# Four edits around one PE-bound mLSTM kernel: quadrants for scaled q, plain transposes for x, a later place for w_out's combinations, one pass on GpSimd

## The chip, the cores and the metric

The kernel runs on 1 core of one Trainium2 chip. The metric is the device time of one execution in microseconds (us), shorter is better; where several runs are at hand, their median. The core has TensorE (PE in the profile, with its weight loads as PEld), VectorE (DVE), ScalarE (ACT), GpSimd (POOL) and SyncE (SP), which issues most DMA transfers. Each engine takes its instructions strictly in its own order, and engines wait for one another through semaphores.

## The reference

Two blocks follow each other. The first is an mLSTM cell with 4 batches, 8 heads, 768 tokens and a head dimension of 40; the second is a feed-forward layer with a leaky ReLU, from 320 to 2048 to 320, on all 3072 tokens.

```python
for t in range(S):
    m_new = max(f[t] + m, i[t]); f_stab = exp(f[t] + m - m_new); i_stab = exp(i[t] - m_new); m = m_new
    C = f_stab * C + i_stab * outer(v[t], k[t])
    n = f_stab * n + i_stab * k[t]
    y[t] = sigmoid(o_gate[t]) * (C @ q[t]) / max(abs(n @ q[t]), 1.0)
x = y.transpose(0, 2, 1, 3).reshape(3072, 320)
h = x @ w_in
out = maximum(0.01 * h, h) @ w_out
```

`w_in` and `w_out` arrive as 64-bit floats. The kernel computes in 32-bit floats, so it narrows the weights itself.

## The kernel before

**Chunks, steps, groups.** The tokens are cut into 6 chunks of 128 (`c`), and a *step* `s = 4 * c + b` is one chunk of one batch. The cell of chunk `c` and the feed-forward layer of chunk `c - 1` (a *group* `g = c - 1` of 4 x 128 = 512 tokens) run side by side. In the cell, q times k gives scores, the scores are weighted with exponentials of the gates, and both the weighted scores and the scaled q (q times the gate's decay) are multiplied into a tile that holds v and the running state.

**Order.** Except for SP, whose transfers have an order chain of their own, the order on every engine is the order of the Python calls. `first_chunk` (L1125) writes out chunk 0: steps 0 and 1, then steps 2 and 3, each with `gate` (L690), `u_x` (L778) and `prepare_step` (L176, GpSimd memsets). The loop at L1244 then walks, per chunk, over the units `ffs[i]` of the feed-forward layer; between them it places the cell's units at fixed places (`place` for chunk 1, `pairs` for the later chunks). Generators are advanced a few instructions at a time: `now` (the narrowing of the weights), `sums` (sums of w_in), `mixes` (combinations of w_out), `lazy` (exponentials), `fine` (transposes of q and k).

**Chunk 1** (steps 4 to 7). For each step `u_split` (L571) turns k and q by matmuls with the identity into the tile `tk`; `u_parts` (L645) first calls `split_qs` (L562), which turns the scaled q (the tile `y`) into `tq`, copied by ScalarE into the tile `qn`; then come the scores `sd` (L662, L667), which VectorE multiplies with the weights into the other half of `qn` (L672) and adds to the state (L643). `u_plain` (L701) multiplies `qn` by v and state into `hN` (L710), takes the denominators, and makes `x` on VectorE (L721) and GpSimd (L726). `ahead(s + 1)` then puts `prep_qs` (L523), `state_next` (L639), `prep_vu` (L514) of the next step and `prep_mask` (L486) of the one after it on GpSimd. When all four steps are done, four `u_x` turn `x` into `xT`, 64 features by tokens in 5 slots of 128 rows: four transposes into the tile `xt`, two matmuls with a 64-column output into `xe`, and three copies.

**fp32 on PE.** In the traces an fp32 matmul shows as two PE instructions, a transpose as one: the 16 matmuls of `split_qs` are 32 in each step, the four transposes of `u_x` are 4 and its two matmuls 4. `split_qs` uses two quadrants of the array in turn (rows 0-63 to columns 64-103, rows 64-127 to columns 0-39); `u_split` uses all four.

**Weights.** `narrow_weights(n)` (L264) makes 32-bit floats of w_in (n = 0 to 3) and w_out (n = 4 to 11, 640 numbers in each of 128 rows) in six passes: two on ScalarE (L272, L273), four on VectorE (bounds L274, shift L277, sign L280, add L281). Those of n = 2 to 11 are drawn in chunk 1 through `now`. Group 0 uses w_in and w_out plainly (L804, L826). The later groups use a scheme with 7 block products instead of 8: `fast_firsts` (L961, matmuls at L977) and `fast_units` (L850, matmuls at L861). It needs sums of w_in (`sums_of_weights`, L932), of x (`sums_of_x`, L951) and of w_out: `mixed_weights` (L220) makes `t3` (L224), the right half of w_out's low rows in place (L225), `t2` (L226) and `t4` (L227).

**PSUM.** Two pools of 4 banks each: `mm` for the feed-forward layer, `c` for the cell.

Of the kernel before, what the change touches and what calls it, by code (L numbers as in the profile page):

```python
# [19 lines left out]
def kernel(  # L20
# [28 lines left out]
    P = 128  # L49
# [6 lines left out]
    D1 = D + 1  # L56
    QW = 32
    DB = D // 2
    V1 = DB + 1
    TB = P // QW  # L60
    SL = P // 2
# [202 lines left out]
    def narrow_weights(n):  # L264

        if not wide:
            return
        raw, dst = raws.pop(n)
        words = raw.bitcast(U32).rearrange("p (c two) -> p c two", two=2)
        lo, hi = words[:, :, 0], words[:, :, 1]  # L270
        d = dst.bitcast(U32)
        yield nc.scalar.activation(dst, hi.bitcast(F32), AF.Abs)  # L272
        yield nc.scalar.activation(lo, lo, AF.Copy, scale=2.0**-29)  # L273
        yield nc.vector.tensor_scalar(  # L274
            dst, dst, scalar1=2.0**-15, scalar2=122879.9921875, op0=ALU.max, op1=ALU.min,
        )
        yield nc.vector.tensor_scalar(  # L277
            d, d, scalar1=0x07FFFFFF, scalar2=3, op0=ALU.bitwise_and, op1=ALU.logical_shift_left,
        )
        yield nc.vector.scalar_tensor_tensor(d, in0=hi, scalar=0xC0000000, in1=d, op0=ALU.bitwise_and, op1=ALU.bitwise_or)  # L280
        yield nc.vector.tensor_tensor(d, d, lo, op=ALU.add)  # L281
# [8 lines left out]
    def gates(c):  # L290


        m0 = m0s.get(c)
        n = P if c == 0 else BH
        fc, il = (f0[:], i0[:]) if c == 0 else (fi[c][:, 0, :], fi[c][:, 1, :])
        F = wk.tile([n, P], F32, name="F", bufs=1)
        nc.vector.tensor_tensor_scan(F[:], fc, zeros[:n].to_broadcast([n, P]), 0.0, op0=ALU.add, op1=ALU.add)
        if c > 0:
            il_t = wk.tile([BH, P], F32, name="il", bufs=1)
            nc.vector.tensor_scalar(il_t[:], il, scalar1=m0[:], scalar2=None, op0=ALU.subtract)  # L300
            il = il_t[:]
        m = wk.tile([n, P], F32, name="m", bufs=1)
        nc.vector.tensor_tensor_scan(m[:], fc, il, -1e30 if c == 0 else 0.0, op0=ALU.add, op1=ALU.max)
        a = early[:, 2, :] if c == 0 else wk.tile([n, P], F32, name="a", bufs=1)
        nc.vector.tensor_tensor(a[:], F[:], m[:], op=ALU.subtract)
        bu = wk.tile([n, 3, P], F32, name="bu", bufs=1)
        nc.vector.tensor_tensor(bu[:, 0, :], il, F[:], op=ALU.subtract)
        if c + 1 < NB:
            m1 = wk.tile([BH, 1], F32, name="m0")
            if c == 0:  # L310
                nc.vector.tensor_copy(m1[:], m[:BH, P - 1 :])
            else:
                nc.vector.tensor_tensor(m1[:], m0[:], m[:, P - 1 :], op=ALU.add)
            m0s[c + 1] = m1
        if c > 0:
            na = wk.tile([BH, 1], F32, name="na")
            nc.vector.tensor_tensor(na[:], m[:, SL - 1 : SL], F[:, SL - 1 : SL], op=ALU.subtract)
        bus[c] = bu, a, (na if c > 0 else None)
# [243 lines left out]
    def split_qs(s):  # L562

        tq = [psc.tile([P, H, SL], F32, name=f"tq{u}", tag="c") for u in range(2)]
        for h in range(H):
            for u, toks, rows in subs(s):
                nc.tensor.matmul(tq[u][rows, h, :], lhsT=st[s]["qs"][toks, h], rhs=ident[toks, toks], start=True, stop=True)  # L567
        for u, toks, rows in subs(s):
            nc.scalar.copy(mixed(s)[rows, u], tq[u][rows])

    def u_split(s):  # L571

# [117 lines left out]
    def gate(s):  # L690

        d = st[s]
        d["x"] = wk.tile([P, Dm], F32, name="x")
        x3 = d["x"][:].rearrange("p (h d) -> p h d", d=D)
        nc.vector.scalar_tensor_tensor(
            x3, in0=d["o"].rearrange("p (h d) -> p h d", d=D), scalar=1.0, in1=d["pa"][:, :, :D],
            op0=ALU.add, op1=ALU.mult,
        )
        nc.vector.tensor_tensor(x3, x3, d["den"][:].unsqueeze(2).to_broadcast([P, H, D]), op=ALU.mult)

    def u_plain(s):  # L701

        c, b = divmod(s, B)
        d = st[s]
        prep_o(s)
        hN = psc.tile([P, H, 2, V1], F32, name="hN", tag="c")
        m = mixed(s)
        for h in range(H):
            for u in range(2):
                nc.tensor.matmul(  # L710
                    hN[ts(u, SL), h].rearrange("p k d -> p (k d)"), lhsT=m[:, u, h, :], rhs=S_v[s % NL][:, u, h, :, :V1],
                    start=True, stop=True,
                )
        state_next(s, 1)
        den = wk.tile([P, H], F32, name="den")
        denominators(den[:], hN[:, :, 0, DB])
        if b < 2:
            d["x"] = wk.tile([P, Dm], F32, name="x")[:]
        else:
            d["x"] = wk.tile([P, H, D1], F32, name="hn")[:].rearrange("p h d -> p (h d)")[:, :Dm]  # L720
        nc.vector.scalar_tensor_tensor(  # L721
            d["x"].rearrange("p (n d) -> p n d", d=DB), in0=natural(s, 2).rearrange("p h (k d) -> p (h k) d", d=DB), scalar=1.0,
            in1=hN[:].rearrange("p h k d -> p (h k) d")[:, :, :DB], op0=ALU.add, op1=ALU.mult,
        )
        x3 = d["x"].rearrange("p (h d) -> p h d", d=D)
        nc.gpsimd.tensor_tensor(x3, x3, den[:].unsqueeze(2).to_broadcast([P, H, D]), op=ALU.mult)  # L726
        state_add(s, 1)

    def u_mix(s):
# [48 lines left out]
    def u_x(s, last=None):  # L778

        c, b = divmod(s, B)  # L780
        d = st[s]
        if b == 0:
            st["xT", c] = wk.tile([P, KC, GT], F32, name="xT", bufs=1)
        xT = st["xT", c]
        xt = psc.tile([P, KC - 1, P], F32, name="xt", tag="c")
        xe = psc.tile([P, P], F32, name="xe", tag="c")
        x, tok = d["x"], ts(b, P)
        for n, at in enumerate((0, P, DP, DP + P)):
            nc.tensor.transpose(xt[:, n, :], x[:, at : at + P], ident[:])  # L789
        for r, at in enumerate((KF * P, 0)):  # L790
            nc.tensor.matmul(xe[ts(r, DP), :], lhsT=x[:, at : at + DP], rhs=ident[:], start=True, stop=True)
        nc.scalar.copy(xT[:, :2, tok], xt[:, :2, :])  # L792
        nc.scalar.copy(xT[:, 2, tok], xe[:])
        (last or nc.scalar.copy)(xT[:, 3:, tok], xt[:, 2:, :])
        if c > 0:
            del st[s]

# [418 lines left out]
    with tc.manual_schedule(engines={E.PE, E.DVE, E.Activation, E.Pool}):  # L1216
# [20 lines left out]
        late = {}  # L1237
        masks = {0: (2, 3), 14: (4, 5)}
        pairs = (1, 1, 3, 3, 13, 13, 17, 17, 17)
        sums = sums_of_weights()  # L1240
        N1 = 14
        now = (None for n in range(2, QN + NF // 2) for _ in narrow_weights(n))
        chores, slow = [], []
        for c in range(1, NB + 1):  # L1244
# [6 lines left out]
            for i in range(n_ff):  # L1251
# [20 lines left out]
                        del fine[min(fine)]  # L1272
                if c == 1 and i >= 24:
                    run(sums, 3)
                if c == 1 and i == n_ff - 2:
                    mixes = mixed_weights()
                if c == 1 and i >= n_ff - 2 or c == 2 and 11 <= i < N1 - 1:
                    next(mixes)
                if i == n_ff - 1 and c < NB:
                    sums_of_x(c)  # L1280
# [74 lines left out]
```

## Time and profile before

| | us |
|---|---|
| median of 3 runs | 490.45 (490.13 to 492.2) |
| profiled execution | 489.68 |
| its span (first to last instruction) | 487.9 |
| PE busy | 476.3 (98% of the span) |
| DVE busy | 334.8 (69%) |
| ACT busy | 202.8 (42%) |
| POOL busy | 176.3 (36%) |

| group of instructions | count | mean ns of one |
|---|---|---|
| L567 PE `tq` (scaled q, 64x40) | 128 | 218 |
| L569 ACT copy `tq` to `qn`, 40x512 | 8 | 579 |
| L789 PE `xt` from `x` | 24 | 377 |
| L791 PE `xe` from `x` | 24 | 399 |
| L274 DVE bounds of w_out, 128x640 | 8 | 679 |
| L224 to L227 DVE combinations of w_out, 128x1280 | 1 each | 1494, 1897, 1485, 2460 |

The matmuls of PE overlap one another, so the time that a stage of PE takes is read from the chain or the timeline (from the start of its first instruction to the start of the next stage), not from the mean of one. The profiled execution is 1.78 us longer than its span, and 0.77 us below the median of the runs. A clock of 1.00 in the profile is the full TensorE clock; the mean granted over the whole execution was 0.983.

### The profile page before, as it was taken

Reading aid. Unit: us, or ns where it says so; the run is one execution under the profiler, and the core shown is the slowest. Engines: PE = TensorE matmul, PEld = TensorE weight load, DVE = VectorE, ACT = ScalarE, POOL = GpSimd, SP = SyncE. Lnnn points to the kernel's source line nnn. Section 1 sums busy time; section 2 is a strip of 40 time slices with the busy share of each in tenths; the row PEclk is TensorE's granted clock in tenths of the full one; section 3 lists DMA queues with packets and bytes.
Section 4 is the critical chain, followed back from the end, with each engine's and each line's share of the span. In section 5 each row is a group of like instructions: output and inputs, shape, how many; then the busy total and the mean of one; then the engine's idle time right before and its main releaser. Section 6 shows DMA issues by size and latency. Waiting matters only on the chain.

```text
span 487.9 us, 14080 instructions
## 1 busy us (share of the span) xinstructions
PE 476.3 (98%) x5685; PEld 428.5 (88%) x5685; DVE 334.8 (69%) x557; ACT 202.8 (42%) x488; POOL 176.3 (36%) x233
## 2 busy tenths in 40 slices
PE   8798999999999999999999999999999999999997
PEld 6676998777678899989899988899989899988997
DVE  3756567699999798888687878688647677104631
ACT  3662498864335631256420345520346411153210
POOL 4311305552376222785113784113773003700020
PEclk9887899999999999999999999999999999999999
DMA  9999686878651584675763775764865212100001
GB/s 122 172 200 210 121 223 179 207 138 173 145 142 28 126 170 83 148 167 122 173 137 88 172 150 123 181 124 90 174 146 126 60 48 68 68 1 1 1 0 55
DMA packets 165040, 59.31 MB, mean 122 GB/s; under 512 B 128560, under 2 KB 155760, under 8 KB 164976
## 3 DMA queue, kind: packets, MB, share of 16 engines
q1 hardware_dynamic: 124944, 51.23, 47.3%
q10 hardware_dynamic: 40032, 7.18, 9.0%
q8 instruction: 45, 0.74, 0.6%
q14 instruction: 19, 0.16, 0.1%
HBM read 51.68 MB, written 6.70 MB: 120 GB/s over the span
## 4 chain that ended last, share of the span: by engine, by line
PE 90%; DMA 4%; SPq 4%; DVE 1%; issue 1%; ACTq 0%; ACT 0%
PE ph L977 32%; PE po L861 32%; PE po L826 7%; PE ph L804 7%; SPq L91 4%; PE pT L740 3%; PE sd L662 3%; DMA acts<-in_moe_w_in_dram 2%; DMA raw<-in_moe_w_in_dram 1%; PE sd L667 1%; PE hN L710 1%; PE tk L581 1%; PE tq L567 1%; PE xt L789 1%; DMA f<-in_f_gate_dram 0%
## 5 line engine op out<-in xcount | busy, mean ns | idle before, releaser
L861 PE MATMUL po<-w_out,acts 128*128 128x160 f32 x640 | 89.1, 300 | 0.0
L861 PEld LDWEIGHTS po<-w_out,acts 128*128 128x128 f32 x640 | 87.3, 190 | 0.6 <-ACT acts L1002 0.3
L977 PE MATMUL ph<-xT,w_in 64*128 64x256 f32 x720 | 82.7, 378 | 0.0
L977 PEld LDWEIGHTS ph<-xT,w_in 64*128 64x128 f32 x720 | 69.3, 187 | 8.8 <-issue 1.1
L1006 DVE TENSOR_TENSOR acts<-acts,ph 128x512 f32<-128x512 f32 x60 | 38.4, 683 | 43.4 <-PE ph L977 43.4
L861 PE MATMUL po<-raw,acts 128*128 128x160 f32 x480 | 66.4, 300 | 0.0
L861 PEld LDWEIGHTS po<-raw,acts 128*128 128x128 f32 x480 | 65.4, 190 | 0.3
L1010 ACT COPY acts<-ph 128x512 f32<-128x512 f32 x60 | 32.1, 586 | 49.1 <-PE ph L977 49.1
L639 POOL TENSOR_TENSOR S<-S,f 40x336 f32<-40x336 f32 x36 | 29.5, 819 | 61.2 <-PE pT L740 26.2
L1002 ACT ACTIVATE acts<-acts 128x1024 f32<-128x1024 f32 x30 | 31.7, 1056 | 44.1 <-DVE acts L1006 33.7
L486 POOL TENSOR_TENSOR w<-w,i 128x512 f32<-128x512 f32 x20 | 26.7, 1340 | 59.5 <-DMA w<-a_dr 41.3
L494 ACT ACTIVATE w<-w,gT 128x64 f32<-128x64 f32 x160 | 41.7, 339 | 10.5 <-DMA w<-a_dr 5.7
L804 PE MATMUL ph<-xT,w_in 64*128 64x256 f32 x320 | 38.5, 395 | 0.7 <-DVE w_in L281 0.7
L672 DVE TENSOR_TENSOR qn<-w,sd 64x512 f32<-64x512 f32 x40 | 27.3, 683 | 15.6 <-ACT acts L1010 4.5
L826 PE MATMUL po<-w_out,acts 128*128 128x320 f32 x128 | 37.1, 441 | 0.0
L977 PE MATMUL ph<-acts,w 64*128 64x256 f32 x320 | 36.6, 381 | 0.0
L804 PEld LDWEIGHTS ph<-xT,w_in 64*128 64x128 f32 x320 | 32.5, 196 | 4.4 <-PE dC L619 0.8
L754 POOL TENSOR_TENSOR xb<-xb,den 128x320 f32<-128x320 f32 x16 | 11.6, 727 | 61.1 <-DVE xb L751 61.1
L977 PEld LDWEIGHTS ph<-acts,w 64*128 64x128 f32 x320 | 30.4, 187 | 3.7
L826 PEld LDWEIGHTS po<-w_out,acts 128*128 128x128 f32 x128 | 23.5, 190 | 9.8 <-issue 1.0
L959 POOL TENSOR_TENSOR acts<-xT 64x256 f32<-64x256 f32 (+1 forms) x30 | 25.5, 862 | 13.0 <-ACT xT L792 9.9
L894 POOL TENSOR_TENSOR y<-y,raw 128x160 f32<-128x160 f32 x10 | 9.4, 944 | 55.8 <-DVE acts L896 45.3
(173 smaller groups left out, 780.0 us busy)
## 6 DMA issues: line engine op xcount, KB each, us to landing
rb<-in_k_dram SPq DMA_DIRECT2D x64, 80.0 KB
rb<-in_q_dram SPq DMA_DIRECT2D x64, 80.0 KB
rb<-in_o_gate_dram SPq DMA_DIRECT2D x64, 80.0 KB
ea<-a_dr SPq DMA_DIRECT2D x32, 128.0 KB
raw<-in_moe_w_out_dram SPq DMA_DIRECT2D x6, 640.0 KB
w<-a_dr ACTq DMA_DIRECT2D x24, 128.0 KB
xT<-x_dr SPq DMA_DIRECT2D x32, 96.0 KB
x_dr<-x SPq DMA_DIRECT2D x64, 40.0 KB
```

Of the source, the lines that this page charges most:

```text
L486: nc.gpsimd.tensor_tensor(w, w, cm2.unsqueeze(1).to_broadcast([P, H, SL]), op=ALU.add)
L494: yield nc.scalar.activation(w[:, h, :], w[:, h, :], AF.Exp, bias=gT[c][:, 0, bh : bh + 1], scale=1.0)
L639: nc.gpsimd.tensor_tensor(new, old, g, op=ALU.mult)
L672: nc.vector.tensor_tensor(mixed(s)[toks, u], w[toks], bank[1 - u][toks], op=ALU.mult)
L804: nc.tensor.matmul(ph[r][:, cols], lhsT=w_row(r, slot, j), rhs=xT[DP * r : DP * (r + 1), slot, cols], start=(slot == 0), stop=(slot == KC ...
L826: nc.tensor.matmul(po[n][:], lhsT=acts[:, f, ts(n, P)], rhs=w_out[:, f, :], start=(f == 0), stop=(f == NF - 1),)
L861: nc.tensor.matmul(bank[:], lhsT=left[:, f, :], rhs=right[:, f, :], start=f == 0, stop=f == KH - 1)
L959: nc.gpsimd.tensor_tensor(to, left, right, op=ALU.subtract)
L977: nc.tensor.matmul(bank[r][:, e, :], lhsT=left(r)[rows, e], rhs=right(r)[rows], start=first and e == 0 and m == 0, stop=e == 1 and m == le ...
L1002: nc.scalar.activation(to, z, AF.Prelu, alpha=0.01)
L1006: nc.vector.tensor_tensor(to[:, 2 * r : 2 * r + 2], to[:, 2 * r : 2 * r + 2], bank[r], op=ALU.add)
L1010: nc.scalar.copy(to[:, 2 * r : 2 * r + 2], bank[r])
```

## The change

1. **`split_qs`:** heads 0 to 3 go to the two quadrants as before, heads 4 to 7 to the other two; the heads are taken in the order 0, 4, 1, 5, 2, 6, 3, 7. ScalarE makes four copies of 40x256 instead of two of 40x512.
2. **`u_x`:** `x` becomes 64 columns wider, and GpSimd copies the first 64 columns behind the last (in `gate` and in `u_plain`). Then slot 2 of `xT` is a plain transpose like the others: five transposes, the first two into one bank (`xt`, now called `low`), three into another (`xe`, now `high`), and two copies, of 128x256 and 128x384.
3. **`narrow_weights`:** for w_out (n = 4 to 11) the pass of the bounds is issued on GpSimd; for w_in it stays on VectorE.
4. **`mixed_weights`:** the first two combinations move from the last two units of group 0 to units 3 and 4 of group 1; the other two stay at units 11 and 12 of group 1.
5. **`gates`:** one subtraction works in place; the tile `il` falls away.

```diff
-        yield nc.vector.tensor_scalar(
+        yield (nc.gpsimd if n >= QN else nc.vector).tensor_scalar(
             dst, dst, scalar1=2.0**-15, scalar2=122879.9921875, op0=ALU.max, op1=ALU.min,
         )
...
-            il_t = wk.tile([BH, P], F32, name="il", bufs=1)
-            nc.vector.tensor_scalar(il_t[:], il, scalar1=m0[:], scalar2=None, op0=ALU.subtract)
-            il = il_t[:]
+            nc.vector.tensor_scalar(il, il, scalar1=m0[:], scalar2=None, op0=ALU.subtract)
...
-        for h in range(H):
+        for h in (0, 4, 1, 5, 2, 6, 3, 7):
             for u, toks, rows in subs(s):
-                nc.tensor.matmul(tq[u][rows, h, :], lhsT=st[s]["qs"][toks, h], rhs=ident[toks, toks], start=True, stop=True)
+                to = rows if h < 4 else slice(SL * u, SL * u + D)
+                nc.tensor.matmul(tq[u][to, h, :], lhsT=st[s]["qs"][toks, h], rhs=ident[toks, toks], start=True, stop=True)
         for u, toks, rows in subs(s):
-            nc.scalar.copy(mixed(s)[rows, u], tq[u][rows])
+            for hs, to in ((slice(0, 4), rows), (slice(4, H), slice(SL * u, SL * u + D))):
+                nc.scalar.copy(mixed(s)[rows, u, hs], tq[u][to, hs])
...
         nc.vector.tensor_tensor(x3, x3, d["den"][:].unsqueeze(2).to_broadcast([P, H, D]), op=ALU.mult)
+        nc.gpsimd.tensor_copy(x[:, Dm:], x[:, :DP])
...
         nc.gpsimd.tensor_tensor(x3, x3, den[:].unsqueeze(2).to_broadcast([P, H, D]), op=ALU.mult)
+        nc.gpsimd.tensor_copy(x[:, Dm:], x[:, :DP])
...
-        xt = psc.tile([P, KC - 1, P], F32, name="xt", tag="c")
-        xe = psc.tile([P, P], F32, name="xe", tag="c")
-        x, tok = d["x"], ts(b, P)
-        for n, at in enumerate((0, P, DP, DP + P)):
-            nc.tensor.transpose(xt[:, n, :], x[:, at : at + P], ident[:])
-        for r, at in enumerate((KF * P, 0)):
-            nc.tensor.matmul(xe[ts(r, DP), :], lhsT=x[:, at : at + DP], rhs=ident[:], start=True, stop=True)
-        nc.scalar.copy(xT[:, :2, tok], xt[:, :2, :])
-        nc.scalar.copy(xT[:, 2, tok], xe[:])
-        (last or nc.scalar.copy)(xT[:, 3:, tok], xt[:, 2:, :])
+        x, xT, tok = st[s]["x"], st["xT", c], ts(b, P)
+        low = psc.tile([P, 2, P], F32, name="xt", tag="c")
+        high = psc.tile([P, KC - 2, P], F32, name="xe", tag="c")
+        for t, n, at in ((low, 0, 0), (low, 1, P), (high, 1, DP), (high, 2, DP + P), (high, 0, 2 * P)):
+            nc.tensor.transpose(t[:, n, :], x[:, at : at + P], ident[:])
+        nc.scalar.copy(xT[:, :2, tok], low[:])
+        (last or nc.scalar.copy)(xT[:, 2:, tok], high[:])
...
-        sums = sums_of_weights()
+        sums, mixes = sums_of_weights(), mixed_weights()
...
-                if c == 1 and i == n_ff - 2:
-                    mixes = mixed_weights()
-                if c == 1 and i >= n_ff - 2 or c == 2 and 11 <= i < N1 - 1:
+                if c == 2 and i in (3, 4, 11, 12):
                     next(mixes)
```

## The prediction

> **What bounds the kernel now.** I read the page's first part, then PE's waits, then the chain of waits in order of time, then the timelines of POOL and DVE at step 5, where the change adds a wait.
>
> ```profile
> PE 476.3 (98%) x5685; PEld 428.5 (88%) x5685; DVE 334.8 (69%) x557; ACT 202.8 (42%) x488; POOL 176.3 (36%) x233
> ```
> ```profile
> PE xt L789 <- DVE x L699: 4.3, 2, 2.6
> PE warm L341 <- POOL ident masks.py:199: 1.5, 1, 1.5
> PE sc L607 <- ACT kqT L598: 1.1, 1, 1.1
> PE sc L607 <- DVE kqT L598: 0.9, 1, 0.9
> PE ph L804 <- DVE w_in L281: 0.7, 1, 0.7
> ```
> ```profile
> 59.34 1.03 PE tk L581 x64
> ...
> 67.10 0.96 PE tq L567 x30
> ...
> 86.66 1.06 PE hN L710 x32
> ...
> 119.43 0.44 PE xt L789 x4
> 119.86 0.37 PE xe L791 x4
> ```
>
> These five waits are all that PE has, and the last ends at 48.88 us. From there to the end the chain is PE alone: a microsecond taken from PE there is won, and one taken from another engine is worth nothing unless PE comes to wait for it. `tk` and `tq` show the prize: 64 instructions in 1.03 us (16.1 ns each) over four quadrants, 30 in 0.96 us (32 ns) over two.
>
> ```profile
> 75.81 0.72 POOL L726 TENSOR_TENSOR x<-x,den 128x320 f32<-128x320 f32 x1 [0.28 <-DVE x L721]
> 76.49 0.97 POOL L523 TENSOR_TENSOR y<-rb,gT 128x320 f32<-128x320 f32 x1
> 77.53 0.90 POOL L639 TENSOR_TENSOR S<-S,f 40x336 f32<-40x336 f32 x1
> 78.51 1.18 POOL L514 TENSOR_TENSOR vu<-kn,gT 128x320 f32<-128x320 f32 x1
> 79.66 1.85 POOL L486 TENSOR_TENSOR w<-w,i 128x512 f32<-128x512 f32 x1
> ```
> ```profile
> 76.23 0.64 DVE L274 TENSOR_SCALAR w_out<-w_out 128x640 f32<-128x640 f32 x1
> 76.91 0.89 DVE L277 TENSOR_SCALAR w_out<-w_out 128x640 uint32<-128x640 uint32 x1
> 77.84 1.27 DVE L280 SCALAR_TENSOR_TENSOR w_out<-w_out 128x640 uint32<-128x640 uint32 x1
> 79.15 1.23 DVE L281 CUSTOM_DVE_ANT_0 w_out<-w_out 128x1280 uint16<-128x1280 uint16 x1
> 83.16 1.40 DVE L672 TENSOR_TENSOR qn<-w,sd 64x512 f32<-64x512 f32 x2 [2.78 <-ACT w L494]
> 84.59 0.50 DVE L643 TENSOR_TENSOR S<-S,sd 40x336 f32<-40x336 f32 x1
> ```
>
> DVE takes the bounds at 76.23, straight after `hN` of step 4; in the new order they stand on POOL behind the five operations above. `hN` of step 5 (86.66) needs L672 and L643, which end at 85.09 behind L281.
>
> **Scaled q in four quadrants.** The same 32 instructions a step, at 16.1 instead of 32 ns: 0.51 us, four times 2.03 us, all on PE's path. Bounds: 2.03, and 0 if the rate stays. I take 2.03; `tk` has the same shapes. On ACT two copies take 1.09 us to the start of the next (81.45 to 82.54); four of half size between 1.08 (four times 0.27, the step from L794 to L494 at 125.75) and 1.5 (four times the 376 ns of a 128x256 copy). Behind them are two exponentials that L672 of step 6 waits for: ready at 97.08, 97.5 at worst; plus 1.93 for L672 and L643 it is 99.0 to 99.4, against `hN` at 99.92 - 0.5 = 99.4: hidden, with no margin at the upper bound (0 to 0.1).
>
> **x by five transposes.** In chunk 1 the stage takes 0.44 + 0.37 = 0.81 us; five transposes at 0.109 are 0.55: 0.26 less, four times 1.0, on PE's path. On ACT three copies become two, with no one behind them; if they were late, the first `ph` of group 1 would wait. In chunk 0 the clock is half (0.50 from 22.4 to 27.7 and 42.0 to 48.8): from 22.49 to 25.80 two stages take 3.31 us; five transposes at 0.25 (four from 22.49 to 23.50) are 1.26, so 0.8 less for steps 0 and 1, and PE has no gap up to 33.0. That reaches 42 through `ph`, ACT, `sc` and `pa`, which follow one another. But the clock comes back at 28.2, inside `ph`: if that moment stays, 0.8 at half speed is worth 0.4. I take 0.5 (0.4 to 0.8). Steps 2 and 3 give nothing: PE waits there for `x` of step 3, and the path is `x`, transposes, DVE's copy, L281, `ph`. Before, the copy ends 1.95 after the transposes start (45.38 to 47.33), having waited for ACT's copy of the same bank; then it has its own bank, 1.26 + 0.05 + 0.55 (0.42 for 256 numbers, 0.13 more) = 1.86.
>
> The Trainium skill, "TensorE: Matmul & The Clock Gate" (What's actually happening), says that the clock is decided in free-running windows of about 3.4 us; this trace changes it at 21.4, 28.2, 41.8 and 52.0, two, four and three such windows apart, and agrees. By that rule the head alone is worth 0.4 and the sum 0.1 less.
>
> **The copy on POOL.** 128x64: 0.23 to 0.29 (a 64x64 copy 0.232, a 128x128 cast 0.293); I take 0.2 between starts. The last transpose waits for it, and behind it PE's next stage; in chunk 0 the other four take 1.0, and in chunk 1 `x` is ready many us ahead. It also stands ahead of `prepare_step`: six memsets, 2.1 us, go from 18.2-20.7 to about 23.6-25.7 and from 40.4-43.1 to about 45.5-47.6. POOL was idle up to 33.27 and 52.80; the transfers of v behind these memsets go out from 43.58 and 61.94.
>
> **Bounds on POOL.** DVE loses eight instructions, 5.4 us; PE waits for DVE nowhere in chunk 1, so that gains nothing. No row has this operation on POOL. Rows with one input tensor give 0.29 for 128 numbers and about 0.95 ns for each further: T = 0.78 us. Rows with two: 0.72 for 320, 1.27 for 512 (L486 at 52.80), so 1.6 for 640; the same L486 beside a busy DVE took 1.86, so 2.3. Below 0.48, DVE's own best, I see no reason to go. I take 0.78, the rows with one tensor.
>
> What waits, in times of before, each step set against its own `hN`: POOL starts `x` of step 4 at 75.81. With DVE idle behind the wait, POOL goes on at its pace of 52.80 to 60.37: 0.68 for `x`, 0.25 for the copy, 0.80 and 0.84 to the next start for L523 and L639, 0.75 and 1.27 for L514 and L486. So L486 ends at 80.4 and the bounds at 80.4 + T. Queued behind the wait on DVE are L277, L280 and L281 (2.33 alone, 85.52 to 87.85; 3.47 beside a busy POOL, above; 2.8 with the second bounds pass beside them), then L672 and L643 (1.93), and `hN` waits for these: 85.1 + T against 86.66 - 0.5 = 86.16. PE stalls if T is above 1.0; at 0.78 the margin is 0.25. Step 6: L643 of step 5 ends at 85.9, or 86.4 on PE's earlier clock; L281 of the second piece at 88.7 instead of 87.85, `x` starts on POOL at 89.9, L486 ends at 94.5, L643 at 99.2 + T, `hN` would start at 99.4: it stalls from T = 0.2, by 0.55 at 0.78. I put 0.5 there (the 0.1 above is in it). Step 7, where DVE had been late and has now less to do: from T = 1.4. Behind POOL's own waits for ACT (L272 at 96.98 and 114.78) stand only state updates, which wait for a later `hN` anyway.
>
> **w_out's combinations.** No transfer and no other queue: 1.49 and 1.90 us of DVE leave 136.8 to 140.1, where PE waits for nothing, and enter behind the L1006 of units 2 and 3 and among the transposes at 159. DVE's gaps ahead of L1006 at 166.60 (2.33) take most of 3.39; L1006 starts 1.06 late and ends at 168.95. The product p3 goes on in that bank at about 169.05 (174.27 less 48 instructions of 0.109). Margin 0.1; without the gap 2.4 more. I put 0.1 (0 to 1.1).
>
> **gates in place.** Five DVE instructions of the same size; nothing.
>
> **Sum.** 2.0 + 1.0 + 0.5 - 0.5 - 0.1 = 2.9 us less: the profiled execution from 489.7 to 486.8 (span 485.0), the median, 0.77 above it, from 490.45 to 487.5.
>
> **The rivals.**
>
> - *POOL becomes the path of chunk 1*, because the bounds cost as much as an operation with two tensors. At T = 1.6 the stalls are 0.6 + 1.4 + 0.2 = 2.2: 489.2. At 2.3 they are 1.3 + 2.1 + 0.9 = 4.3: 491.3, slower than before; it decides at about T = 2.0. If L277 to L281 also took 3.47 each time, 0.67 more at three steps: 493.3. For: L486 grew from 1.27 to 1.86, and there is next to no margin. Against: at the places that count DVE waits, so POOL works alone, and the bounds read one tensor.
> - *The first bounds pass on POOL costs microseconds once more than the others*, as an operation that POOL had not run. It decides from an extra of 0.25 + 2.9 = 3.2 us; at 5 the time is 492.3. Against: the first cast (0.29) and the first L504 (0.72) took what the later ones took; ACT's table load, the nearest row of a loading, took 1.28, which would leave 488.5. The Trainium skill, "GPSIMD Engine Reference" (2.1 Instruction dispatch), gives about 6 us for the first call of a freshly loaded kernel, by which it would be 493.2; no row here shows it.
> - *Four quadrants don't pay for tq* (the change doesn't do what it says): 2.0 less gain, 489.5. Against: `tk`.
> - *Another wait on PE*, at p3 or for a transfer that comes no earlier though PE does: 1 to 2 us, 488.5 to 489.5.
>
> **How the numbers follow.** The forecast holds with 0.56; its own range is 486.2 to 488.0: 0.5 more stall above, and below no stalls and up to 0.7 from the 3.1 us at half speed that PE has after 48.88. POOL's path has 0.17 (of it 0.05 above 492.9), another wait 0.14, tq 0.08, the first pass 0.05 (above 492.9 from an extra of 5.7, nearly all of it). About 0.5% (2.45 us) is what a measurement of this kernel can tell from no change: faster 0.56, slower 0.09, same 0.35. The range, 486.0 to 490.8, reaches over tq, other waits and most of POOL's path.
>
> **What would show it.** Right: `tq` stages of 0.5 us; transposes of 0.55 without `xe`'s matmuls; no PE wait after 49 us but some 0.5 ahead of `hN` of step 6; the wait of `ph` at 48.88 some 0.5 earlier; bounds on POOL near 0.8; DVE idle ahead of L277 of the first piece for about 5 us. Wrong: PE waiting over 1 us ahead of `hN` of steps 5 to 7, a first bounds pass above 4 us, `tq` still near 1 us, or L977 waiting for L1006.

## The result: 1% slower, where 0.6% faster was forecast

| kernel | median us (range, runs) | ratio to the kernel before, 95% interval |
|---|---|---|
| before | 490.44 (490.13 to 492.2, 6) | 1 |
| changed | 495.43 (493.94 to 495.91, 6) | 1.0091 [1.0067, 1.0115] |

The changed kernel is about 4.5 to 5 us slower. Its profiled execution took 494.9 us (span 493.1), the one of before 489.68 (487.9). Three of the runs used below took 6 to 7 us more at a lower granted clock (0.965 or 0.966; two of the kernel before, one of the fastest kernel): ratios leave them out, medians do not.

From the page of the changed kernel, its first part (busy us, share of the span, instructions):

```profile
PE 473.1 (96%) x5661; PEld 426.7 (87%) x5661; DVE 326.5 (66%) x549; ACT 202.7 (41%) x488; POOL 197.3 (40%) x249
```

PE's work did become less, by 3.2 us, and DVE's by 8.3; POOL has 21.0 us more. A span that grows by 5.2 us while PE works 3.2 less means that PE does nothing for 8.4 us more. PE's waits in the changed kernel (engine, line, releaser: us in all, times, longest):

```profile
PE xt L787 <- DVE x L700: 6.1, 2, 3.5
PE hN L712 <- DVE S L644: 3.0, 3, 1.0
PE hN L712 <- DVE qn L673: 2.0, 2, 1.3
PE ph L799 <- DVE w_in L282: 1.9, 2, 1.0
```

Before the change the second and the third of these were not there, and the first and the fourth were 4.3 and 0.7. The 5.0 us ahead of `hN` lie in steps 5 to 7. The chain of waits through step 6 and into the stage behind step 7 (start, length, what):

```profile
94.38 1.24 POOL w L485
95.62 2.32 POOL w_out L275
...
97.97 1.01 DVE w_out L278
...
99.00 0.84 DVE w_out L281
...
100.81 0.68 DVE qn L673
...
101.52 0.69 DVE qn L673
...
102.25 0.50 DVE S L644
...
112.55 2.32 POOL w_out L275
...
120.68 1.11 PE hN L712 x30
121.79 3.98 PE po L821 x8
```

The chain has left PE. It goes through POOL's queue (the mask L485, then the bounds L275, here 2.32 us), from there to DVE's shift (L278) and the passes behind it, and only then to L673 and L644, which `hN` waits for. And the last stage, eight instructions of `po`, takes 3.98 us where it took 2.35 before:

```profile
117.08 2.35 PE po L826 x8
...
120.23 4.50 PE po L826 x16
```

The changed kernel at the same place by windows (from and to, then length and each engine's busy time with its count, granted clock, DMA share, GB/s):

```profile
118.30:121.70 3.40, 1.67 (x34) 1.20 (x32) 3.30 (x6) 0.00 (x0) 3.20 (x3) 0.99 0.72 147
121.70:125.10 3.40, 3.40 (x9) 2.19 (x8) 3.23 (x6) 0.00 (x0) 0.91 (x1) 0.51 0.76 151
125.10:128.50 3.40, 3.40 (x17) 2.56 (x16) 3.22 (x9) 2.24 (x8) 0.54 (x1) 1.00 0.81 177
```

PE was busy for only 1.67 of the first 3.40 us; in the next 3.4 us the clock that it is granted is half. So here the stall is paid for twice, once as the wait and once as 1.6 us of slow work behind it. The groups of the bounds pass on POOL and of the pass behind it on DVE (busy us, mean ns of one, then idle time before):

```profile
L275 POOL TENSOR_SCALAR w_out<-w_out 128x640 f32<-128x640 f32 x8 | 19.8, 2486 | 0.0
...
L278 DVE TENSOR_SCALAR w_out<-w_out 128x640 uint32<-128x640 uint32 x8 | 6.5, 816 | 18.5 <-POOL w_out L275 18.5
```

Seven of the eight passes take 2.33 to 2.34 us on POOL, three of them while VectorE stands waiting for them; the fifth (at 100.21 us) takes 3.51, and why is not shown. The first took no longer than the others, so the rival of a dear first pass is out. The prediction took T = 0.78 us and had 2.3 as the upper end.

The two gains on PE are there. From the chain, `tq` of step 4 and the first stage of transposes of chunk 1 in the changed kernel:

```profile
67.41 0.59 PE tq L567 x32
...
125.77 0.22 PE xt L787 x2
125.99 0.33 PE xe L787 x3
126.32 4.31 PE po L821 x16
```

`tq` fell from 0.96 to 0.59 us, the transposes from 0.81 to 0.55. One thing was not forecast: the `po` stage behind the transposes fell too, from 4.50 (the line of before above) to 4.31.

### The profile page after: what moved, and what is told of

Its sections match the earlier page's. It is cut to its first block, busy times and chain, and to the rows that moved or that the text cites. A ratio compares the mean times of both kernels' runs of the same rounds, so it can differ in the third digit from the quotient of the medians.

```text
span 493.1 us, 14032 instructions
## 1 busy us (share of the span) xinstructions
PE 473.1 (96%) x5661; PEld 426.7 (87%) x5661; DVE 326.5 (66%) x549; ACT 202.7 (41%) x488; POOL 197.3 (40%) x249
## 4 chain that ended last, share of the span: by engine, by line
PE 81%; DMA 6%; SPq 5%; DVE 3%; POOL 3%; issue 1%; ACT 0%; ACTq 0%; DVEq 0%; POOLq 0%
PE ph L972 32%; PE po L856 31%; SPq L92 5%; PE ph L799 5%; PE po L821 4%; PE pT L740 3%; PE sd L663 3%; DMA kn<-in_k_dram 3%; DMA acts<-in_moe_w_in_dram 3%; POOL w_out L275 1%; DVE w_out L278 1%; PE sd L668 1%; DMA rb<-in_k_dram 1%; DVE qn L673 1%; DVE w_out L281 1%
## 5 line engine op out<-in xcount | busy, mean ns | idle before, releaser
L640 POOL TENSOR_TENSOR S<-S,f 40x336 f32<-40x336 f32 x36 | 30.2, 838 | 46.6 <-PE pT L740 26.1
L485 POOL TENSOR_TENSOR w<-w,i 128x512 f32<-128x512 f32 x20 | 26.6, 1338 | 54.2 <-DMA w<-a_dr 35.6
L821 PE MATMUL po<-w_out,acts 128*128 128x320 f32 x128 | 38.3, 452 | 0.0
L673 DVE TENSOR_TENSOR qn<-w,sd 64x512 f32<-64x512 f32 x40 | 27.3, 683 | 12.3 <-ACT acts L1005 5.2
L889 POOL TENSOR_TENSOR y<-y,raw 128x160 f32<-128x160 f32 x10 | 10.2, 1020 | 55.0 <-DVE acts L891 45.2
L954 POOL TENSOR_TENSOR acts<-xT 64x256 f32<-64x256 f32 (+1 forms) x30 | 23.6, 801 | 12.4 <-ACT xT L788 9.5
```

Source lines behind the costliest of these rows:

```text
L485: nc.gpsimd.tensor_tensor(w, w, cm2.unsqueeze(1).to_broadcast([P, H, SL]), op=ALU.add)
L640: nc.gpsimd.tensor_tensor(new, old, g, op=ALU.mult)
L673: nc.vector.tensor_tensor(mixed(s)[toks, u], w[toks], bank[1 - u][toks], op=ALU.mult)
L821: nc.tensor.matmul(po[n][:], lhsT=acts[:, f, ts(n, P)], rhs=w_out[:, f, :], start=(f == 0), stop=(f == NF - 1),)
```

## The experiments

Three theories were to be told apart. **A:** the length of the bounds pass on POOL is the loss, and without it the other parts gain. **B:** the wider x (POOL's copy, five transposes) or the four copies of `tq` lose too. **C:** the place of w_out's combinations loses. All ratios are to the kernel before, run on the same chip; two chips were used, and the medians of the kernel before lie between 490.36 and 490.73 us.

### One part at a time

**Bounds back on VectorE**, all else as changed:

```diff
-        yield (nc.gpsimd if n >= QN else nc.vector).tensor_scalar(
+        yield nc.vector.tensor_scalar(
```

> The changed kernel with part 3 undone: w_out's bounds go back to VectorE; all else stays. Theory (the bounds pass takes 2.3 us on GpSimd and stands on the way to hN of steps 5 to 7, about 5.0 us of waits, and the stop at step 7 costs about 1.6 us more at half clock): no wait of PE ahead of hN of steps 5 to 7, no stretch at half clock behind hN of step 7, and 488 to 489 us, 6 to 7 less than the changed kernel and 1.5 to 2.5 less than the one before. Rival 1 (the four ScalarE copies of tq or GpSimd's added copy of x delay the chain to qn, and the bounds only show where it is waited for): waits ahead of hN of over 2 us remain, 491 to 493. Rival 2 (the combinations of w_out in group 1 are the larger loss): 492 or more, with the loss at about 180 us.

Measured: 489.88 us, ratio 0.9987 [0.9973, 1.0002]. The waits ahead of `hN` are gone, and so is the half clock behind `hN` of step 7. So the bounds cost the changed kernel 495.43 - 489.88 = 5.5 us. (Between the two profiles steps 4 to 7 differ by 5.0 us of stalls and 1.6 of half clock. The profile of the changed kernel, though, comes to `tk` of step 4 2.9 us earlier, at 59.56 against 62.47 us, because it spent less time at half clock up to there. With 0.6 us more in group 1 the spans differ by 4.3.) But what is left is not the 488 to 489 that theory A expected: another part loses as well.

**Bounds on POOL alone**, added to the kernel before by the same line:

> The kernel before with part 3 alone: w_out's bounds on GpSimd. Theory (the pass is the cause by itself): 2.3 us for each of the eight, PE waits ahead of hN of steps 5 to 7 of about 1.0, 1.8 and 1.2 us (a little less than in the changed kernel, since PE comes to hN 0.4 us later in each step without the quadrants), with or without a half clock behind the last; 494.5 to 497 us. Rival 1 (the delay needs GpSimd's copy of x or the four copies of tq): waits under 1.5 us in all, under 492.

Measured: 494.07 us, 1.0071 [1.0052, 1.0091], 3.7 us over before and just under the range expected; PE's waits:

```profile
PE hN L710 <- DVE S L643: 2.4, 3, 1.0
...
PE hN L710 <- DVE qn L672: 0.5, 1, 0.5
```

The waits sum to 2.9 us instead of 5.0; by the stretches from `tk` (in step 7 from `tg`) to `hN`, steps 5 to 7 are 0.66, 1.94 and 1.36 us longer than before, 4.0 as expected (1.1 of it stands in no row of waits). There is no half clock behind step 7 (`hN` to `xt` 3.28 us, before 3.33). With `tq` slow, PE comes to each `hN` 0.4 us later: in the changed kernel the gain from `tq` was partly turned into a longer wait.

**Quadrants alone** (part 1 of the diff on the kernel before):

> The kernel before with part 1 alone: scaled q in four quadrants and four ScalarE copies. Theory: tq takes 0.5 to 0.6 us a step and each step is 0.4 us shorter up to the end of the scores; 488.4 to 489.0 us, no new wait of PE. Rival 1 (four copies on ScalarE delay the exponentials that qn waits for): PE waits ahead of hN of step 6, 489.5 to 490.5.

Measured: 489.17 us, 0.9976 [0.9963, 0.9989], 1.2 us under before and between the two ranges; the prediction's term was 2.0. From one `tk` to the `hN` behind it a step is 0.35 to 0.44 us shorter, but behind `hN` of step 6 there is a new wait, of `tg` for DVE. ACT and DVE in this kernel, from the timelines:

```profile
95.73 1.54 ACT L571 COPY qn<-tq 40x256 f32<-40x256 f32 x4
97.17 0.59 ACT L494 ACTIVATE w<-w,gT 128x64 f32<-128x64 f32 x2
```
```profile
97.79 1.40 DVE L674 TENSOR_TENSOR qn<-w,sd 64x512 f32<-64x512 f32 x2 [3.40 <-ACT w L494]
```

Four copies take 1.44 us to the start of the next operation (two took 1.08), the two exponentials behind them end at 97.76, L674 starts at 97.79, and DVE runs late from there: the stretch from `tk` of step 7 to `tg` is 3.86 us instead of 3.38. That returns 0.48 of the 1.6 us.

**Five transposes alone** (part 2, with the subtraction in place of part 5):

> The kernel before with part 2 (and the subtraction in place of part 5, which makes the room): x 64 columns wider, GpSimd's copy, five transposes, two copies. Theory: four stages in chunk 1 are 0.26 us shorter each and the feed-forward products behind them 0.2 us shorter each, 1.8 us in all; the head ends between 0.5 us earlier and 0.3 us later (its clock comes back later); 488.2 to 489.6 us. Rival 1 (GpSimd's copy of x delays the chain to hN by itself): a wait of PE ahead of hN of steps 5 or 6 of over 0.3 us, 490 or more. By the prediction's own terms (1.0 in chunk 1, 0.5 in the head) 488.9.

Measured: 492.57 us, 1.0033 [1.0013, 1.0053]. This part alone makes the kernel 1.6 (by the ratio) to 2.2 us (by the medians) slower. In its profile (493.53 us, the slowest of the nine runs) the four stages of chunk 1 (from the first `xt` to the first `ph` of group 1) took 17.36 instead of 19.17 us, the expected 1.8, but three other places lost more: `tk` of step 4 comes 2.84 us later than in the profile of before, the stretch from `tk` of step 7 to `tg` is 0.97 longer (0.81 of it a gap in `po` that the profile puts to no releaser), and that from the first `ph` of group 1 to `tg` of the next chunk 1.8 longer (below, at w_out's combinations). Neither the theory nor its rival had that.

### Where the five transposes lose: the head

In the head, PE's stages in the kernel with the bounds on VectorE (new head), from the timeline:

```profile
25.93 0.60 PE L596 MATMUL tkq<-ident,qn 128*128 128x128 f32 x4
27.82 2.43 PE L799 MATMUL ph<-xT,w_in 64*128 64x256 f32 x20 [1.28 <-DVE w_in L282]
...
35.82 4.12 PE L799 MATMUL ph<-xT,w_in 64*128 64x256 f32 x20
```

The transposes end earlier, and then PE stands 1.28 us waiting for w_in's first piece (L282): DVE's passes over it decide when `ph` can start. And `ph` at 35.82 takes 4.12 us: half clock. So chunk 0 alone was put back to the old transposes (and with them GpSimd's copy left out there, so that the two are not told apart):

```diff
     def gate(s):
...
-        nc.gpsimd.tensor_copy(x[:, Dm:], x[:, :DP])
...
     def u_x(s, last=None):
...
+        if c == 0:
+            for n, at in enumerate((0, P, DP, DP + P)):
+                nc.tensor.transpose(xt[:, n, :], x[:, at : at + P], ident[:])
+            for r, at in enumerate((KF * P, 0)):
+                nc.tensor.matmul(xe[ts(r, DP), :], lhsT=x[:, at : at + DP], rhs=ident[:], start=True, stop=True)
...
+        else:
             for t, n, at in ((low, 0, 0), (low, 1, P), (high, 1, DP), (high, 2, DP + P), (high, 0, 2 * P)):
                 nc.tensor.transpose(t[:, n, :], x[:, at : at + P], ident[:])
...
```

> The changed kernel with w_out's bounds back on VectorE and, in chunk 0 alone, x transposed as before (four transposes, two 64-column matmuls, three copies, no copy on GpSimd); chunks 1 to 5 keep the five transposes. Theory A (the five transposes are right in chunk 1, 1.8 us, and what they lose in the only-transposes kernel and in the one with the bounds on VectorE is the head: PE then waits for the first piece of w_in instead, and the clock stays at half for about two windows more): the mean granted clock is 0.979 to 0.983 as before, instead of 0.976, and the time 487 to 488.5 us, 1.5 to 2.5 less than with the new head. Rival B (the loss lies in chunk 1 and behind it, where VectorE and ScalarE are late): 489.5 to 490.5, as with the new head. Rival C (the clock's windows fall by chance and not by the head's form): the clock as with the new head, 0.976, and 489 to 490.

Measured: 487.93 us (487.39 for the five runs of the ratio), 0.9950 [0.9931, 0.9970]. Theory A of this run holds: 1.95 us less than with the new head, and the two intervals don't meet. This is the lowest median of the study, 2.5 us under before. By landmarks of its profile against that of before: `tk` of step 4 0.38 later, steps 4 to 7 0.95 shorter, the four stages of transposes 1.81 shorter, the rest equal; sum -2.4, and the spans differ by 2.4. The clock in the new head and in this one, in stretches of 3.4 us:

```profile
32.70:36.10 3.40, 2.32 (x37) 2.04 (x33) 2.73 (x7) 3.40 (x6) 1.56 (x4) 1.00 0.90 122
36.10:39.50 3.40, 3.40 (x18) 2.79 (x18) 2.22 (x5) 0.35 (x1) 0.20 (x2) 0.50 1.02 243
```
```profile
31.90:35.30 3.40, 2.29 (x53) 2.01 (x53) 2.70 (x6) 3.40 (x10) 1.08 (x3) 1.00 0.93 123
35.30:38.70 3.40, 3.40 (x36) 2.74 (x32) 2.98 (x6) 1.68 (x2) 0.86 (x3) 1.00 1.10 231
```

The first fence (bounds on VectorE, new head) has one full window at half clock, the second (old head) has none there. In every profile of the study the half-clock stretches up to 60 us are 3.4, 6.8, 10.2 or 13.6 to 13.7 us long: one to four windows of 3.41. One such window is 1.7 us of PE's full-speed work, and 0.0035 of the mean clock of an execution. By that measure the runs with the new head and the bounds on VectorE had a mean of 0.976 in most cases (seven windows at half), those with the old head and the bounds on VectorE 0.979 (six), and those of before 0.983 or 0.979 (five or six) about equally often.

Where the loss lies can be read from the profiles. From the first `xt` to the first `ph` they take 5.0 us with the new head and 5.0 to 5.2 with the old one, so nothing is lost there. From the first `ph` to `tk` of step 4 the six profiles with the old head (without extra matmuls) take 31.5 to 33.0 us, 10.2 to 13.7 of them at half clock; the six with the new head take 32.2 to 34.8, with 10.2 to 17.3 at half clock. Without half of the time at half clock all twelve are 26.1 to 27.3 us. So the head loses by the clock and not by the wait for L282. It is also a matter of where the windows lie: at the same mean clock of 0.979 the three runs with the new head average 489.5 us and the four with the old one 488.1.

**The changed kernel with only the head put back**, bounds on POOL:

> The changed kernel, bounds on GpSimd, with x of chunk 0 transposed as before. Theory (the head's loss and the bounds' loss add): 493 to 494 us, 1.5 to 2.5 under the changed kernel and 5 to 6 over the same kernel with the bounds on VectorE (487.9); the mean clock one window above the changed kernel's (0.979). Rival (the head costs the changed kernel nothing, since its profile is only 0.3 us late at tk of step 4): 495 to 496.

Measured: 493.48 us, 1.0071 [1.0049, 1.0092]. The difference to the changed kernel is 1.95 us by medians but only 1.0 by the ratios, and the intervals overlap for more than half of their length; the six runs fall into two groups, near 492.3 and near 494.8, at one mean clock, which no trace explains. So this pair agrees with the loss of the head and doesn't show it by itself. To the same kernel with the bounds on VectorE the difference is 5.55: the bounds lose as much with the one head as with the other. The profile of the changed kernel alone hid the loss of the head: in that execution the head had five windows at half, so `tk` of step 4 was only 0.3 us late, while the mean clock of most of its other runs, 0.976, means one window more; no trace shows where it lies.

**Does a waiting PE bring the clock down?** Eight matmuls of the identity with itself ahead of `u_x(0)` and ahead of `u_x(3)`, in the kernel with the old head:

```diff
         gate(1)
+        warm(8)
         u_x(0)
...
         gate(3)
+        warm(8)
         u_x(3, on_v)
```

> The kernel with the head as before, plus eight matmuls of the identity with itself ahead of x of step 0 and eight ahead of x of step 3, where PE waits for VectorE. Their output is used by nothing. Theory A (a PE that stands still in the head is what brings the clock down to half): fewer half-speed windows, a mean granted clock of 0.986 or more, and 2 to 4 us less than the same kernel without them. Rival C (the clock falls for another reason than the waits): clock unchanged, time the same or up to 0.5 us longer.

Measured: mean clocks of 0.985 to 0.999, and 488.14 us, 0.9959 [0.9936, 0.9982]: the clock went up and the median did not go down. Among the twelve runs the clock and the time do go together: the five with 0.996 or more have a median of 486.7 us, the four with 0.985 or 0.986 one of 489.1. With the first eight only:

> The kernel with the old head, bounds on VectorE and the other parts (487.9), plus eight matmuls of the identity with itself ahead of x of step 0 alone; nothing uses their output. Theory (PE's standing still brings the clock down, but the first piece of w_in, ready on VectorE at about 27.3 us, sets when the first ph starts; the second eight only delayed x of step 3): the clock is back by 23 us instead of 28, the first ph starts 0.5 to 0.7 us earlier, and 486.5 to 488. Rival (a full clock in the head is worth as much as the half clock costs there, 3 to 4 us): 484 to 485.

Measured: 488.63 us, 0.9965 [0.9942, 0.9987], above the range of the theory and far from that of the rival. In its profile the clock is back at 21.8 instead of 28.5 us, and then:

```profile
25.58 0.60 PE L596 MATMUL tkq<-ident,qn 128*128 128x128 f32 x4
27.95 2.43 PE L810 MATMUL ph<-xT,w_in 64*128 64x256 f32 x20 [1.77 <-DVE w_in L282]
```

PE reaches `ph` at full clock and waits 1.77 us for w_in: `ph` starts 0.22 us earlier than without the extra matmuls (28.17), not 0.5 to 0.7. Filling the waits brings the clock up (shown), but up to the first `ph` a faster PE gains next to nothing, since w_in's first piece is the path. What a half window costs depends on where it lies: ahead of that `ph` two windows cost the 0.22 us, behind it one costs up to 1.7. The second eight of the other kernel, at half clock, took 3.6 us and themselves delayed the transposes of step 3. No gain over the kernel without them is shown.

That waiting is what brings the clock down is not shown. In the kernel before, PE was busy throughout the window ahead of 41.82 us (32 instructions of `pa`), and the clock fell to half all the same:

```profile
38.41:41.82 3.41, 3.41 (x32) 3.41 (x32) 1.46 (x6) 1.37 (x4) 1.02 (x3) 1.00 1.17 224
41.82:45.23 3.41, 1.88 (x11) 1.15 (x10) 2.90 (x6) 0.91 (x3) 0.77 (x2) 0.50 1.06 210
```

And the kernel with the first eight matmuls had a window with PE busy for only 1.64 us (25.20 to 28.61) and kept the full clock behind it. So in the head the busy time that the profile counts doesn't tell what the next window gets. In chunk 1 it does as far as these profiles go: windows with PE busy for 1.05 to 1.69 us (the changed kernel and two others with the bounds on POOL) were followed by one at half clock, windows with 1.85 us and more (two of them in stalls of step 6) were not.

### The price of the pass, and whether the price is all

Four forms of the pass on POOL in one kernel:

```diff
+        if n in (4, 5):
+            yield nc.gpsimd.tensor_scalar(
+                dst, dst, scalar1=2.0**-15, scalar2=122879.9921875, op0=ALU.max, op1=ALU.min,
+            )
+        elif n in (6, 7):
+            yield nc.gpsimd.tensor_scalar(dst, dst, scalar1=2.0**-15, scalar2=None, op0=ALU.max)
+        elif n in (8, 9):
+            nc.gpsimd.tensor_scalar(
+                dst[:, :Dm], dst[:, :Dm], scalar1=2.0**-15, scalar2=122879.9921875, op0=ALU.max, op1=ALU.min,
+            )
...
+        elif n >= QN:
+            yield nc.gpsimd.tensor_copy(dst, dst)
...
```

> The changed kernel with four forms of the bounds pass on GpSimd, two pieces of w_out each: maximum and minimum as now (2.3 us), maximum alone, maximum and minimum in two halves of 320 numbers, and a plain copy in place. It leaves out the upper bound for two pieces and both bounds for two more. Theory A (each of the two operations is paid for each number): maximum alone about 1.2 us, the halves 1.16 to 1.2 us each, the copy 0.6 to 0.8. Theory B (this form costs 3.6 ns for each number whatever it does): maximum alone 2.3 us, the copy alone cheaper. In both the total is 1 to 4 us under the changed kernel, since some of the passes are shorter.

POOL's timeline of this kernel (start, length, line, operation; "x2" is two in a row):

```profile
80.54 4.66 POOL L276 TENSOR_SCALAR w_out<-w_out 128x640 f32<-128x640 f32 x2
...
95.92 3.58 POOL L280 TENSOR_SCALAR w_out<-w_out 128x640 f32<-128x640 f32 x2
99.47 1.29 POOL L282 TENSOR_SCALAR w_out<-w_out 128x320 f32<-128x320 f32 x1
...
114.82 0.71 POOL L289 COPY w_out<-w_out 128x640 f32<-128x640 f32 x1
```

Two operations 2.33 us, one 1.79, halves 1.26 to 1.29, a copy 0.71 to 0.78. Neither theory was right: a `tensor_scalar` with one operation is already 2.5 times a copy of the same size, and the second operation adds 0.54. From 320 to 640 numbers the price goes from 1.27 to 2.33, so 3.3 ns for each number and about 0.2 us fixed. The time of this kernel, 494.97 us, says nothing more: the long forms came first, and PE's waits ahead of `hN` are 5.4 us here.

Then the prediction's own value of T was put in: a plain copy for all eight pieces, with every wait and every place kept.

```diff
-        yield (nc.gpsimd if n >= QN else nc.vector).tensor_scalar(
-            dst, dst, scalar1=2.0**-15, scalar2=122879.9921875, op0=ALU.max, op1=ALU.min,
-        )
+        if n >= QN:
+            yield nc.gpsimd.tensor_copy(dst, dst)
+        else:
+            yield nc.vector.tensor_scalar(
+                dst, dst, scalar1=2.0**-15, scalar2=122879.9921875, op0=ALU.max, op1=ALU.min,
+            )
```

> The changed kernel with all eight bounds passes on GpSimd replaced by a plain copy in place of the same 128x640 numbers (measured at 0.71 to 0.78 us); the waits and the places on each queue stay. It leaves out the bounds. Theory (the length of the pass alone makes the stalls; the prediction's chain of waits holds once T is 0.78): PE waits ahead of hN of steps 5 to 7 of 0 to 0.8 us in all instead of 5.0, no half clock behind hN of step 7, and 489.5 to 491 us, 4.5 to 6 under the changed kernel. Rival (the handing over from ScalarE to GpSimd to VectorE costs, whatever the pass takes): over 2 us of waits remain, 492 or more.

Measured: 489.82 us, 0.9987 [0.9973, 1.0000], 5.6 us under the changed kernel and level with the bounds on VectorE (489.88). POOL's group, and what PE still waits for ahead of `hN`:

```profile
L276 POOL COPY w_out<-w_out 128x640 f32<-128x640 f32 x8 | 5.6, 722 | 5.2 <-ACT w_out L273 5.2
```
```profile
PE hN L715 <- DVE S L647: 0.2, 1, 0.2
```

With T = 0.72 the waits go from 5.0 to 0.2 us. Handing the piece from ACT to POOL to DVE costs nothing that can be measured here; the length of the pass is the loss.

### The place of w_out's combinations

**The move alone**, on the kernel before:

```diff
-                if c == 1 and i == n_ff - 2:
-                    mixes = mixed_weights()
-                if c == 1 and i >= n_ff - 2 or c == 2 and 11 <= i < N1 - 1:
+                if c == 2 and i in (3, 4, 11, 12):
                     next(mixes)
```

> The kernel before with part 4 alone: w_out's first two combinations moved into group 1. Theory (the place of the combinations matters only where PE runs ahead of VectorE; before the change neither place is on PE's path, and 0.1 was the prediction's term): 490.1 to 490.7. Rival (VectorE gets late at the additions of units 3 and 4 of group 1): a gap of 0.5 to 1.1 us among the products or po of group 1 between 166 and 185 us, 491 to 491.5.

Measured: 490.62 us, 1.0009 [0.9992, 1.0025]: nothing that can be measured, as expected.

**The move undone** in the kernel with quadrants, five transposes and the bounds on VectorE:

> The changed kernel with part 3 and part 4 undone: bounds on VectorE, w_out's combinations in their old place at the end of group 0. Theory (in the only-transposes kernel PE waited about 1.1 us around 152 us, because VectorE, with the combinations still ahead of it, no longer kept up with a PE that is 1.8 us earlier): the same wait of 1 to 2 us between the first products of group 1 and its first po, and 0.5 to 1.5 us more than with the combinations moved (about 490.5 to 491.5). Rival (the place of the combinations does nothing, or costs the 0.6 us that the prediction allowed): 489.3 to 490.0.

Measured: 491.17 us, 1.0017 [1.0005, 1.0029], 1.3 more than with the combinations moved. DVE and PE in the old place, from the timelines:

```profile
140.80 1.92 DVE L225 TENSOR_TENSOR raw<-w_out 128x1280 f32<-128x1280 f32 x1
142.76 1.90 DVE L226 TENSOR_TENSOR w_out<-w_out 128x1280 f32<-128x1280 f32 x1
```
```profile
150.73 1.15 PE L740 MATMUL pT<-qn,S 128*64 128x64 f32 x32 [0.55 <-DVE S L644]
152.56 1.15 PE L740 MATMUL pT<-qn,S 128*64 128x64 f32 x32 [0.68 <-DVE S L644]
```

With PE 1.8 us earlier in group 0, DVE, which has L225 and L226 ahead of the gates and of L644, is late for `pT` of chunk 2 by 1.2 us. Moved, the two stand where DVE has room. So the move is worth nothing by itself and 1.3 us in company; that it is part 2 that calls for it is what the kernel with five transposes alone suggests, where the same stretch was 1.8 us longer, while with the quadrants alone it was not. Theory C falls.

### The parts together

| part | alone, us | in company, us |
|---|---|---|
| bounds on POOL | +3.7 | +5.5 (two pairs: 495.43 - 489.88, 493.48 - 487.93) |
| x by five transposes | +2.2 | head +1.95 (two pairs, the second not clear of noise); chunk 1 -1.8 (profiles) |
| quadrants for scaled q | -1.2 | steps 4 to 7: -0.95 (profile of the fastest kernel) |
| w_out's combinations moved | 0 (+0.2, within the interval) | -1.3 |

In company the parts give 5.5 + 1.95 - 1.8 - 0.95 = +4.7, against 4.5 to 5.0 measured (the -1.8 was read with the combinations moved, so the -1.3 is not taken off again). The first two terms are differences of the same medians, so only the last two put the sum to the test. The kernels that keep both gains without the two losses are the one with the old head and the bounds on VectorE, 487.93, and its two forms with extra matmuls.

## Why the prediction was wrong

**The term that failed: "I take 0.78, the rows with one tensor".** T was 2.33 (3.51 once in eight). The working behind it held: it said that PE stalls in step 5 from T = 1.0, and gave for T = 2.3 stalls of 1.3, 2.1 and 0.9 us. Against the kernel with the bounds on VectorE, the changed one lost 1.30 in step 5, 2.24 in step 6 and 1.6 from there to `hN` of step 7. And with T set to 0.72 the loss is gone. The mistake was to order the rows by how many tensors they read. The 0.78 was drawn out from rows of 64 and 128 numbers, copies and casts; for a copy it held (0.72 for 640 numbers), but maximum and minimum cost 3.2 times a copy, and the only computing rows with one input were two selects of 128x128 (0.29, as much as a cast). The evidence on the page was for an unknown between 0.48 and 2.3, and with a decision point at about 2.0 the chance of 0.17 for this rival was too small. The rival named the place and the way of the loss, and gave 491.3. That its T of 2.3 was right to 0.1 is luck: it was the price of two tensors beside a busy DVE, with 1.6 for POOL alone, and the pass took 2.33 with DVE standing still.

**What that rival lacked** for the 4 us from 491.3 to 495.4. First the half clock behind the stall at step 7, 1.6 us: PE busy for 1.67 of 3.4 us, then a window at half. The prediction used the clock's windows for the head alone, and a new stall can meet them too. The Trainium skill, "TensorE: Matmul & The Clock Gate" (What's actually happening), has the clock set by how busy PE was in free-running windows of about 3.4 us. The 3.41 us of these profiles agree with the windows. With "how busy" the profile's busy time agrees in chunk 1 only: in the head a window with PE busy throughout was followed by half clock (at 41.82 us before). Second the head, below.

**"x by five transposes ... head 0.5".** It went the other way by about 2 us. Two steps failed. The first is "PE has no gap up to 33.0": in the profile of before PE had none because it reached the first `ph` at 27.70, after w_in's first piece, which ended on DVE at 27.05. In the changed kernel PE was through with the work ahead of `ph` at 26.42, the piece ended at 27.27 and `ph` began at 27.41: of 1.3 us only 0.3 was left, and the rest became a wait for L282, in the profiles with the new head of 0.8 to 1.3 us. That takes away most of the gain and makes no loss. The second step makes it: the prediction took the clock's windows as they were before but for the moment at 28.2, and put no loss on them. The runs with the new head have about one window more at half clock, which the profiles show behind the first `ph`. Why is not shown: in the new head a window with PE busy for 2.32 of 3.4 us was followed by one at half clock, in the old head one with 2.29 was not. Whether a transpose counts for the clock as the matmuls that it replaces do, no run tells.

**"x by five transposes ... chunk 1, 1.0".** The mechanism held, the size was 1.8: four times 0.26 for the transposes and four times 0.19 for the `po` behind them. In a stage after matmuls with 64 output columns `po` took 4.50 us, after a plain transpose 4.31. Why is not shown.

**"Scaled q in four quadrants, 2.03".** The rate held nearly (0.59 instead of 0.51 us), the gain from `tk` to `hN` is 0.35 to 0.44 a step. The term for the four copies, "hidden, with no margin at the upper bound", came out at that bound (1.44 us for four, bounds 1.08 and 1.5), and the stretch after `hN` of step 6 paid 0.48 for it; 1.2 us were left.

**"The copy on POOL 0.2"**: 0.24 in six of eight and 0.71 and 0.77 in two, with no wait of PE put down to it. **w_out's combinations, 0.1:** 0 alone. That their old place would cost 1.3 us once PE is earlier was not seen; the prediction asked only what the new place costs.

**The sum.** 2.0 + 1.0 + 0.5 - 0.5 - 0.1 became 1.0 + 1.8 - 1.95 - 5.5, which is 4.7 us more instead of 2.9 less. Two places decided it. At step 5 the margin of 0.25 us was trusted with an unknown larger than it. In the head neither the margin of 0.65 us at the first `ph` nor a change of the clock's windows was asked about.

## What to carry to other kernels

When a pass moves to an engine where the trace has no row of the same operation, do not price it by a copy: here even the computing row with two tensors gave only 1.6 us for what took 2.33. Ask what the upper end does to the first instruction that waits behind it, or measure the one instruction first. A gain on the bounding engine counts only up to the next input that this engine needs; look for the instruction that was ready just ahead of it before. And a wait on PE can cost a second time, as a window at half clock behind it: in chunk 1 it did where PE was busy for half a window or less.

## What the runs showed of the hardware that was not expected

- GpSimd, 128x640 fp32 in place: copy 0.71 to 0.78 us, `tensor_scalar` with one operation 1.79, with two 2.33 (the fifth of eight 3.51, in three kernels alike); 128x320 with two 1.27.
- A stall of 1.7 us in a 3.4 us window at 118.3 to 121.7 was followed by exactly one window at half clock, 68 us behind the last one before it. A window with PE busy throughout (38.41 to 41.82 before) was followed by three.
- Half-clock stretches in all fourteen profiles are whole multiples of 3.41 us. Extra matmuls raised the mean clock from 0.979 to 0.985 or more and did not lower the median (488.14 against 487.93 us), though among their runs the higher clocks go with the shorter times.
- `po` stages of 16 instructions took 4.31 us behind five plain transposes and 4.50 behind transposes and two 64-column matmuls.
